# Second products of a two-layer pipeline taken out of the steps of the first products

## The chip, the core and the metric

The kernel runs on one core of a Trainium2 chip. TensorE (PE in the profile, its weight loads PEld) does the matrix products out of SBUF into PSUM; VectorE (DVE), ScalarE (ACT) and GpSimd (POOL) work on tiles in SBUF and PSUM; SyncE (SP) issues nearly all transfers. Each engine works through its own list of instructions in order, and semaphores tie the lists together. The metric is device time in microseconds (us), and less is better. Before the change three runs gave 1913.86, 1925.21 and 1925.63 us, with a median of 1925.21.

## The reference

Three stages, all in float32, over 8 sequences of 576 positions (4608 tokens, width 512):

```python
scores = scale * q @ k.T                  # 8 heads of 64
ret = scores * Dmat                       # Dmat = gamma[h] ** (i - j) for i >= j, else 0
x = ret @ v                               # 4608 x 512

h = x @ w_in                              # first MLP: 512 -> 2048
g = h * (1.0 / (1.0 + np.exp(-1.702 * h)))
x = g @ w_out                             # 2048 -> 512

h = x @ w_in2                             # second MLP
g = h - np.tanh(h)
out = g @ w_out2
```

## The kernel before

**Three passes.** A product of two float32 matrices is made of three: each operand is split into a high part in float32r and the rest, and the pairs high-high, high-low and low-high are added up in PSUM (`PASS`). A split costs one copy on ACT and one subtraction on DVE.

**Steps.** Tokens are cut into 9 blocks of 512, the 2048 inner columns into 16 groups of 128. One step of an MLP is one block and one group, 144 steps for each MLP and 288 in all (MLP 1 has 0 to 143, MLP 2 has 144 to 287). A step has a *first product* (x by w_in, 12 matmuls of 512 columns, `mm_in`, L419, or L618 and L632 in MLP 2), an *activation* (ACT and DVE, result in the tile `t`), a store of `t` to DRAM (`g_store`, L455), later a load of it (`g_load`, L463, tile `gl`), a split (`act_b`, ACT L468 and DVE L469, tile `g`) and a *second product* (g by w_out, four units of three matmuls, `mm_out`, L485 in MLP 1 and L487 in MLP 2). Its w_out rows come from DRAM (`wo_load`, L200, 512 KB, tile `wos`, three buffers). After 16 second products a block is done and `evac` copies the four PSUM accumulators out (L503).

**What runs beside what.** Retention (`attn_step`, a batch every other step) feeds the first product. The second product of step o runs in the program step of the first product s = o + 32, from s = 32 to s = 143. Beside it go the decoding of the weights from 64-bit floats (`dec_piece`), then `w2_prep`, which stores the combinations of w_in2 that are used later (DVE `ws` L563, POOL L585), and from s = 90 on nothing of the decoding is left. Then the first block of MLP 2 is multiplied plainly (`mm_std`, L618, 16 steps, activation `act_2`). The other 8 blocks go in four pairs, by a scheme with 7 half-size products in place of 8: for each of 8 groups q the parts 1, 6, 5, 2, 7, 3, 4 (`mm_part`, L632, 6 matmuls each) yield four h tiles. Parts 1 and 2 share the PSUM bank x, 5 and 3 bank y, 7 and 4 bank z, and 6 has bank w; x and w lie in one PSUM tile, `pat`. Part results are copied (m1, m7, h22 on ACT) and added (u2, h12, h21 on DVE, h22 on POOL). Between the parts `some(outs, n)` hands out n units of second products, 16 units (four steps) for each q, so that at the end 32 steps of second products remain. For each pair the operands of the next are made (`xo_prep`: POOL L640, ACT L543, DVE L544).

**Order.** The program is written in its final order, and a tile that is allocated takes the buffer that comes free. In a program step the loads for the second product come ahead: `out_loads(o)` asks for w_out and for `gl` of step o + 2, `act_b` is one step ahead, and `stores(2)` stores the activation of two steps ago:

```python
        out_loads(o)
        mm_in(s)
        if s % 2 == 0 and EARLY + BPB + (s - LAG) // 2 <= TILES * BPT:
            attn_step(EARLY + BPB + (s - LAG) // 2)
        dec_piece()
        act_a(s)
        act_b(o + 1)
        done.append(s)
        stores(2)
        for m in range(4):
            mm_out(o, m)
```

The tile `t` has three buffers, `gl` two, `g` two, and a first product's PSUM tile `h` two.

Of the kernel before, what the change touches and what calls it, by code (L numbers as in the profile page):

```python
# [17 lines left out]
P = 128  # L18
# [24 lines left out]
GDS = 6 * NF  # L43
# [5 lines left out]
def kernel(  # L49
# [16 lines left out]
    at_p = ctx.enter_context(tc.tile_pool(name="at", bufs=2))  # L66
# [10 lines left out]
    qt_sb = const.tile([P, KD, P], F32, name="qt_sb")  # L77
    mt_sb = const.tile([P, BPT, 2, 2, P], F32, name="mt_sb")
    mk_sb = const.tile([P, P], F32, name="mk_sb")
    jt_sb = const.tile([P, HEADS], F32, name="jt_sb")  # L80
    kt_sb = const.tile([P, 2, HEADS, 1], F32, name="kt_sb")
    gt_sb = const.tile([P, HP], F32, name="gt_sb")
# [3 lines left out]
    sbd = [const.tile([P, 2, P], F32, name=f"sbd{bt}") for bt in range(BPT)]  # L86
    s_sb = [const.tile([P, 2, HD], F32, name=f"s_sb{bt}") for bt in range(BPT)]
# [345 lines left out]
    def act_2(s, h):  # L433

        tt[s] = t = t_p.tile([P, BLK], F32, tag="t", name="t", bufs=3)
        sq = t_p.tile([P, BLK], F32, tag="e", name="sq")
        pl = t_p.tile([P, BLK], F32, tag="z", name="pl", bufs=3)
        if not marks:
            marks["t"] = at_p.tile([P, 4, BLK], F32, tag="at", name="marks")
            marks["n"] = 0  # L440
        small = marks["t"][:, marks["n"] % 4]
# [11 lines left out]
    def g_store(s):  # L453
        gd[s] = dram.tile([P, BLK], F32, tag=f"g{s % GDS}", name="gd")
        nc.sync.dma_start(out=gd[s], in_=tt.pop(s))  # L455

    def g_load(s):
        if s < (2 * NB - 2) * NF:
            t = t_p.tile([P, BLK], F32, tag="gl", name="gl")
        else:  # L460
            t = st_p.tile([P, BLK], F32, tag="stg", name="gl", bufs=3)
        gl[s] = t
        nc.sync.dma_start(out=t, in_=gd.pop(s))  # L463

    def act_b(s):
        t = gl.pop(s)
        gt[s] = g = g_p.tile([P, 2, BLK], F32R, tag="g", name="g")
        nc.scalar.activation(out=g[:, 0], in_=t, func=ACTF.Copy)  # L468
        nc.vector.tensor_tensor(out=g[:, 1], in0=t, in1=g[:, 0].bitcast(F32), op=ALU.subtract)  # L469
# [19 lines left out]
    def evac(s):  # L489
# [3 lines left out]
        if j >= NB - 2:  # L493
            o = at_p.tile([P, 4, BLK], F32, tag="at", name="o")
            parts = [o[:, m] for m in range(4)]
        else:
            parts = [p_p.tile([P, BLK], F32, tag="p", name="o") for m in range(4)]
        for m in range(4):
            r = (j - NB) * BLK + m * P
# [5 lines left out]

    def out_loads(o):
        if o + 2 < n_steps:
            wo_load(o + 2)
            last = (2 * NB - 2) * NF
            for u in (o + 2,) if o + 2 < last else (last, last + 1) if o + 2 == last else (o + 3,):  # L510
                if u < n_steps:
                    g_load(u)

    def out_units(first, last):

        for o in range(first, last):
            out_loads(o)
            if o + 1 < n_steps:
                act_b(o + 1)
            for m in range(4):  # L520
                mm_out(o, m)
                if m == 3:
                    if o % NF == NF - 1:
                        evac(o)
# [216 lines left out]
    for i in range(NF):  # L741
# [9 lines left out]
        if i == NF - 1:  # L751
            act_b(0)
# [8 lines left out]
        if NF - 5 <= i < NF - 3:  # L761
            wo_load(i - NF + 5)
            g_load(i - NF + 5)

    n_steps = 2 * NB * NF
# [13 lines left out]
    xo_tag += [f"wi{f}" for f in range(NF)] + ["ws", "ws"]  # L779
    for s in range(LAG, NB * NF):  # L780
        j, f = divmod(s, NF)
        o = s - LAG
        out_loads(o)
        mm_in(s)
        if s % 2 == 0 and EARLY + BPB + (s - LAG) // 2 <= TILES * BPT:
            attn_step(EARLY + BPB + (s - LAG) // 2)
        dec_piece()
        act_a(s)
        act_b(o + 1)
# [5 lines left out]
        if f == NF - 1:  # L795
            evac(o)
# [7 lines left out]
    outs = out_units(NB * NF - LAG, n_steps)  # L804
# [3 lines left out]
    for i in range(NF):  # L808
# [4 lines left out]
        some(outs, 1)  # L813
        act_2(s, h)
        done.append(s)
        stores(2)
        some(outs, 3)
# [8 lines left out]
    for p in range(pairs):  # L826
# [6 lines left out]
        for q in range(QS):  # L833
# [7 lines left out]

            x_ps, w_ps = pat[:, 0], pat[:, 1]
            mm_part(x_ps, q, 1, True)
            if late:
                late[0]()
            some(outs, 2)
            if late:
                late[1]()
            stores(2)
            ready()  # L850

            m1 = p_p.tile([P, BLK], F32, tag="p", name="m1")
            nc.scalar.activation(out=m1, in_=x_ps, func=ACTF.Copy)  # L853
            mm_part(w_ps, q, 6, True)
            some(outs, 2)
            u2 = p_p.tile([P, BLK], F32, tag="p", name="u2")
            nc.vector.tensor_tensor(out=u2, in0=w_ps, in1=m1, op=ALU.add)
            ready()
            y_ps = ps_h.tile([P, BLK], F32, tag="h", name="y")
            mm_part(y_ps, q, 5, True)  # L860
            some(outs, 2)
            if late:
                late[2]()
            stores(2)
            ready()

            h22 = p_p.tile([P, BLK], F32, tag="p", name="h22")
            nc.scalar.activation(out=h22, in_=y_ps, func=ACTF.Copy)  # L868
            nc.gpsimd.tensor_tensor(out=h22, in0=u2, in1=h22, op=ALU.add)  # L869
            mm_part(x_ps, q, 2, False)  # L870
            some(outs, 2)
            act_2(ids[0] + q, x_ps)
            done.append(ids[0] + q)
            ready()
# [3 lines left out]
            stores(2)  # L878
# [96 lines left out]
```

## Time and profile before

| | |
|---|---|
| median of three runs | 1925.21 us |
| profiled execution, device time | 1926.46 us |
| its span, first to last instruction | 1924.6 us |
| mean granted TensorE clock | 0.961 of full speed |
| busy: PE, DVE, ACT, POOL | 92%, 62%, 45%, 13% of the span |
| transfers | 514 MB, mean 267 GB/s |
| chain of waits, by engine | PE 50%, DMA 16%, DVE 16%, ACT 10% |

The page's busy share of PE counts a matmul from its issue to its end, and neighbours overlap; how fast PE really goes is seen in how many matmuls start in a stretch. The chain of waits is followed back from the last instruction: DMA, DVE and ACT have 42% of it, though PE is the engine with the most work.

### The profile page before, as it was taken

The page shows a single profiled execution, that of the slowest core. Times are in us where ns is not written, and L with a number is a line of the kernel's source. Part 1 is how long each engine was busy: PE and PEld are TensorE (multiplying, and loading weights), DVE is VectorE, ACT ScalarE, POOL GpSimd, SP SyncE. Part 2 cuts the span into 40 slices and gives each one's busy share as a digit, 9 for nine tenths or more (in the row PEclk, how much of TensorE's full clock was granted, in tenths as well). Part 3 has the DMA queues.
Part 4 walks back from the last instruction along what each step waited for, and adds up shares of the span by engine and source line. Part 5 has one row for each costly group of instructions (what it writes and reads, how often), then busy time and mean ns, then how long its engine had stood idle before and what let it go on. Part 6 is the DMA issues. An engine that isn't in the chain of part 4 may idle for free.

```text
span 1924.6 us, 24809 instructions
## 1 busy us (share of the span) xinstructions
PE 1764.3 (92%) x8714; PEld 1412.2 (73%) x8714; DVE 1184.0 (62%) x1837; ACT 872.3 (45%) x1587; POOL 252.5 (13%) x185
## 2 busy tenths in 40 slices
PE   7998999999999999999988897988888888988898
PEld 5786888888788888888766676766666666767677
DVE  6798865666633333334656787767766777766632
ACT  3344432343423233224554566555555656555522
POOL 4011000101011111000200211121111211111100
PEclk8999999999999999999989998999988998999999
DMA  6559998888989787889968776777677677777843
GB/s 238 170 196 331 368 328 294 283 317 298 322 282 306 261 284 267 274 274 367 387 247 293 246 256 243 252 241 255 232 250 261 238 239 243 268 251 242 324 147 110
DMA packets 176029, 514.23 MB, mean 267 GB/s; under 512 B 19873, under 2 KB 21025, under 8 KB 164385
## 3 DMA queue, kind: packets, MB, share of 16 engines
q1 hardware_dynamic: 164960, 493.69, 73.8%
q10 hardware_dynamic: 10944, 18.96, 2.6%
q8 instruction: 69, 1.13, 0.2%
q14 instruction: 56, 0.45, 0.1%
HBM read 380.45 MB, written 132.12 MB: 266 GB/s over the span
## 4 chain that ended last, share of the span: by engine, by line
PE 50%; DMA 16%; DVE 16%; ACT 10%; issue 6%; ACTq 0%; SPq 0%; POOL 0%; DVEq 0%; POOLq 0%
PE acc L485 17%; PE h L419 16%; DMA gl<-gd 11%; PE acc L487 6%; DVE g L469 4%; DMA gd<-t 4%; ACT pl L446 2%; DVE pl L449 2%; DVE pl L450 2%; ACT sq L445 2%; PE pat L632 2%; PE pat L287 2%; DVE t L444 2%; ACT t L443 1%; ACT g L468 1%
## 5 line engine op out<-in xcount | busy, mean ns | idle before, releaser
L485 PE MATMUL acc<-g,wos 128*128 128x512 f32 x1728 | 431.6, 397 | 20.4 <-DVE g L469 11.5
L487 PE MATMUL acc<-wos,g 128*128 128x512 f32 x1398 | 380.2, 408 | 55.0 <-DVE g L469 38.4
L485 PEld LDWEIGHTS acc<-g,wos 128*128 128x128 f32 x1728 | 322.8, 190 | 99.2 <-DVE g L469 15.3
L419 PE MATMUL h<-xh,wi 128*128 128x512 f32 x1152 | 380.8, 394 | 6.4 <-DVE t L429 4.8
L487 PEld LDWEIGHTS acc<-wos,g 128*128 128x128 f32 x1398 | 275.1, 198 | 133.6 <-DVE g L469 51.8
L469 DVE TENSOR_TENSOR g<-gl,g 128x512 fp32r<-128x512 f32 x288 | 258.8, 906 | 181.2 <-ACT g L468 180.6
L468 ACT ACTIVATE g<-gl 128x512 fp32r<-128x512 f32 x288 | 180.1, 626 | 310.8 <-PE acc L487 143.1
L419 PEld LDWEIGHTS h<-xh,wi 128*128 128x128 f32 x1152 | 218.9, 190 | 55.0 <-DVE t L429 5.4
L419 PE MATMUL h<-xl,wi 128*128 128x512 f32 x576 | 226.6, 393 | 0.7 <-DVE xl L353 0.7
L429 DVE SCALAR_TENSOR_TENSOR t<-t,h 128x512 f32<-128x512 f32 x144 | 98.5, 684 | 193.7 <-ACT t L428 193.1
L632 PE MATMUL pat<-xo,wq 128*128 128x512 f32 x576 | 159.6, 415 | 53.2 <-ACT m L853 53.2
L632 PEld LDWEIGHTS pat<-xo,wq 128*128 128x128 f32 x576 | 110.7, 197 | 89.3 <-ACT m L853 67.0
L428 ACT ACTIVATE t<-h 128x512 f32<-128x512 f32 x144 | 85.2, 593 | 190.5 <-DMA gd<-t 100.0
L449 DVE SCALAR_TENSOR_TENSOR pl<-pl,sq 128x512 f32<-128x512 f32 x144 | 99.5, 691 | 99.1 <-ACT pl L446 98.9
L451 DVE COPY_PREDICATED t<-marks,pl 128x512 f32<-128x512 int32 x144 | 134.1, 931 | 14.8
L244 POOL TENSOR_TENSOR at<-at,qt_sb 128x512 f32<-128x512 f32 x35 | 47.6, 1361 | 625.0 <-DMA at<-in_attn_dram 517.7
L419 PEld LDWEIGHTS h<-xl,wi 128*128 128x128 f32 x576 | 109.4, 190 | 23.4 <-DVE xl L353 1.0
L353 DVE TENSOR_TENSOR xl<-pat,xh 128x256 fp32r<-128x256 f32 x61 | 25.8, 423 | 163.0 <-ACT xh L352 163.0
L112 ACT ACTIVATE e<-e,ebias 128x512 int32<-128x512 int32 x64 | 46.3, 724 | 173.9 <-DVE e L110 173.9
L869 POOL TENSOR_TENSOR h<-u,h 128x512 f32<-128x512 f32 x32 | 46.7, 1460 | 577.5 <-ACT h L868 577.5
L632 PE MATMUL z<-xo,wq 128*128 128x512 f32 x384 | 111.8, 432 | 0.0
L446 ACT ACTIVATE pl<-sq,abias 128x512 f32<-128x512 f32 x144 | 104.2, 723 | 4.7
(92 smaller groups left out, 2121.7 us busy)
## 6 DMA issues: line engine op xcount, KB each, us to landing
wos<-wd SPq DMA_DIRECT2D x262, 512.0 KB, 4.8
gd<-t SPq DMA_DIRECT2D x288, 256.0 KB, 5.1
gl<-gd SPq DMA_DIRECT2D x288, 256.0 KB, 4.4
wq<-wq SPq DMA_DIRECT2D x48, 1024.0 KB, 7.5
at<-in_attn_dram SPq DMA_DIRECT2D x33, 1024.0 KB, 6.3
stg<-in_w_dram SPq DMA_DIRECT2D x64, 512.0 KB, 6.8
wq<-wq SPq DMA_DIRECT2D x32, 768.0 KB, 9.1
wd<-ws SPq DMA_DIRECT2D x32, 512.0 KB, 6.5
```

Of the source, the lines that this page charges most:

```text
L244: eng.tensor_tensor(out=qv, in0=qv, in1=qt_sb[:, hp], op=ALU.mult)
L419: nc.tensor.matmul(h, lhsT=win[f][:, a, k], rhs=xs[b][:, k], start=(n == 0), stop=(n == 3 * KD - 1))
L428: nc.scalar.activation(out=t, in_=h, func=ACTF.Tanh, scale=0.851)
L429: nc.vector.scalar_tensor_tensor(out=t, in0=t, scalar=1.0, in1=h, op0=ALU.add, op1=ALU.mult)
L446: nc.scalar.activation(out=pl, in_=sq, func=ACTF.Square, bias=abias)
L449: nc.vector.scalar_tensor_tensor(out=pl, in0=pl, scalar=CB, in1=sq, op0=ALU.add, op1=ALU.mult)
L451: nc.vector.copy_predicated(out=t, mask=small.bitcast(I32), data=pl)
L468: nc.scalar.activation(out=g[:, 0], in_=t, func=ACTF.Copy)
L469: nc.vector.tensor_tensor(out=g[:, 1], in0=t, in1=g[:, 0].bitcast(F32), op=ALU.subtract)
L485: nc.tensor.matmul(acc[m], lhsT=wo[:, a, c], rhs=g[:, b], start=first, stop=last)
L487: nc.tensor.matmul(acc[m], lhsT=g[:, a, c], rhs=wo[:, b], start=first, stop=last)
L632: nc.tensor.matmul(ps, lhsT=wq[q][t][:, o, a, k], rhs=xo[i][k][:, b], start=first and n == 0, stop=n == 5, skip_group_check=True,)
```

## The change

1. The second products become one generator, `out_units()`, from step 0. The program steps up to s = 89 (`PAUSE = 90`) still hand out four units each; the 54 steps from s = 90 to 143 hand out none.
2. The 54 missing steps are made up later: 22 steps instead of 16 beside `mm_std`, and 22 units instead of 16 (5.5 steps) for each q of the pairs. 32 steps remain at the end, as before.
3. In the pairs the parts go 1, 5, 7, 6, 2, 3, 4, each followed by three or four units; the copies of banks x, y and z (m1, h22, m7) are issued right after their part; u2 and both POOL additions follow part 6; the activations of the last group are spread over the next.
4. Once retention is over (s = 126), its tables and buffers give way to a pool that adds three buffers for `t`, two for `gl`, one for `g` and four for outputs. From then on `gl` is loaded four steps ahead, and `act_b` is two ahead.
5. `marks`, a mask of `act_2`, has two rows in place of four, and each stored activation has a DRAM tile of its own.

```diff
+    second = {}
+    turns = {"t": 0, "gl": 0, "g": 0}
+    def turn(what):
+        shape, dt, n = {"t": ([P, BLK], F32, 3), "gl": ([P, BLK], F32, 2), "g": ([P, 2, BLK], F32R, 2)}[what]
+        i = turns[what]
+        turns[what] += 1
+        more = {"t": 3, "gl": 2, "g": 1}[what]
+        if second and i % (n + more) >= n:
+            return second["pool"].tile(shape, dt, tag=what + "2", name=what, bufs=more)
...
     def out_loads(o):
         if o + 2 < n_steps:
             wo_load(o + 2)
...
+        while n_g[0] <= min(o + (4 if second else 2), n_steps - 1):
+            g_load(n_g[0])
+            n_g[0] += 1
+    def out_split(o):
+        while n_b[0] <= min(o + (2 if second else 1), n_steps - 1):
+            act_b(n_b[0])
+            n_b[0] += 1
+    def out_units():
+        for o in range(n_steps):
             out_loads(o)
+            out_split(o)
             for m in range(4):
                 mm_out(o, m)
...
+    outs = out_units()
     for s in range(LAG, NB * NF):
         j, f = divmod(s, NF)
         o = s - LAG
-        out_loads(o)
+        if s < PAUSE:
+            out_loads(o)
         mm_in(s)
...
         act_a(s)
-        act_b(o + 1)
+        if s < PAUSE:
+            out_split(o)
         done.append(s)
         stores(2)
-        for m in range(4):
-            mm_out(o, m)
+        if s < PAUSE:
+            some(outs, 4)
...
         mm_std(s, h, s % NF)
-        some(outs, 1)
+        some(outs, 2)
         act_2(s, h)
         done.append(s)
-        stores(2)
-        some(outs, 3)
+        stores(3)
+        some(outs, 3 + half_)
...
             mm_part(x_ps, q, 1, True)
+            m1 = copied(x_ps, "m1")
             if late:
+                h21 = added(late["z"], late["u2"], "h21")
+            some(outs, 3)
             if late:
+                act(late["id"][1] + QS, late["h22"])
             y_ps = ps_h.tile([P, BLK], F32, tag="h", name="y")
             mm_part(y_ps, q, 5, True)
+            h22 = copied(y_ps, "h22")
+            ready()
+            some(outs, 3)
             if late:
+                act(late["id"][0] + QS, late["h12"])
             z_ps = ps_h.tile([P, BLK], F32, tag="h", name="z")
             mm_part(z_ps, q, 7, True)
+            m7 = copied(z_ps, "m7")
+            ready()
             some(outs, 3)
+            mm_part(w_ps, q, 6, True)
+            u2 = added(w_ps, m1, "u2")
+            nc.gpsimd.tensor_tensor(out=h22, in0=u2, in1=h22, op=ALU.add)
+            nc.gpsimd.tensor_tensor(out=h22, in0=h22, in1=m7, op=ALU.add)
             ready()
+            some(outs, 3)
+            if late:
+                act(late["id"][1], h21)
+            mm_part(x_ps, q, 2, False)
+            ready()
+            some(outs, 3)
+            act(ids[0] + q, x_ps)
             mm_part(y_ps, q, 3, False)
+            h12 = added(y_ps, u2, "h12")
+            ready()
+            some(outs, 3)
             mm_part(z_ps, q, 4, False)
+            some(outs, 4)
```

`copied` and `added` are one ACT copy and one DVE addition out of PSUM into a new tile; `act` is `act_2`, then `stores(3)`.

Three places where the change moves instructions. First SP's list, two program steps, s = 50 and 51, before (wd_1583 and wd_1645 are rows of w_out, `gd` stored activations):

```order
L200 DMA wos_2779<-wd_1583 128x1024
L463 DMA gl_2781<-gd_1036 128x512
L236 DMA at_2812<-in_attn_dram 128x2048
L159 DMA wr_2816<-z_2647 128x512
L100 DMA stg_2818<-in_w_dram 128x512
L455 DMA gd_2828<-t_2706 128x512
L200 DMA wos_2847<-wd_1645 128x1024
L463 DMA gl_2849<-gd_1085 128x512
L455 DMA gd_2871<-t_2758 128x512
```

and two steps, s = 48 and 49, of the list after the change:

```order
L202 DMA wos_2699<-wd_1538 128x1024
L476 DMA gl_2701<-gd_916 128x512
L457 DMA gd_2747<-t_2613 128x512
L202 DMA wos_2749<-wd_1538 128x1024
L161 DMA wr_2767<-z_2609 128x512
L102 DMA stg_2769<-in_w_dram 128x512
L202 DMA wos_2773<-wd_1553 128x1024
L476 DMA gl_2775<-gd_965 128x512
L457 DMA gd_2801<-t_2659 128x512
L202 DMA wos_2803<-wd_1553 128x1024
```

Each row of w_out is now loaded twice in a step, since `out_loads(o)` is called by the loop and again by the generator: 320 loads of `wos` in place of 262, the 58 more in the steps s = 32 to 89. Only the second of the two tiles is read. In the built program the load that is read, or the one ahead of it, waits for the second product of the same step o; before the change the only load waited for that of step o - 1.

Second, PE's list for most of one group q of a pair, before (acc is a second product, pat bank x or w):

```order
L632 MATMUL pat<-xo,wq 128x512 x6
L487 MATMUL acc_13390<-wos,g 128x512 x3
L487 MATMUL acc_13394<-wos,g 128x512 x3
L632 MATMUL pat<-xo,wq 128x512 x6
L487 MATMUL acc_13419<-wos,g 128x512 x3
L487 MATMUL acc_13423<-wos,g 128x512 x3
L632 MATMUL y<-xo,wq 128x512 x6
```

and after the change, from part 1 to part 2 of a group:

```order
L651 MATMUL pat<-xo,wq 128x512 x6
L500 MATMUL acc_11099<-wos,g 128x512 x3
L500 MATMUL acc_11103<-wos,g 128x512 x3
L500 MATMUL acc_11107<-wos,g 128x512 x3
L651 MATMUL y<-xo,wq 128x512 x6
L500 MATMUL acc_11132<-wos,g 128x512 x3
L500 MATMUL acc_11099<-wos,g 128x512 x3
L500 MATMUL acc_11103<-wos,g 128x512 x3
L651 MATMUL z<-xo,wq 128x512 x6
```

Part 6, which stood two units behind part 1 in the same PSUM tile, now stands behind parts 5 and 7 and nine units. Third, DVE's list in one group of a pair after the change, from the activation of h12 to the start of that of bank x:

```order
L446 TENSOR_TENSOR t<-h_9988,t 128x512
L451 SCALAR_TENSOR_TENSOR pl<-pl,sq 128x512
L452 SCALAR_TENSOR_TENSOR pl<-pl,h_9988 128x512
L453 COPY_PREDICATED t<-marks,pl 128x512
L482 TENSOR_TENSOR g<-gl,g 128x512
L877 TENSOR_TENSOR u_10140<-pat,m_10038 128x512
L446 TENSOR_TENSOR t<-h_10040,t 128x512
L451 SCALAR_TENSOR_TENSOR pl<-pl,sq 128x512
L452 SCALAR_TENSOR_TENSOR pl<-pl,h_10040 128x512
L453 COPY_PREDICATED t<-marks,pl 128x512
L482 TENSOR_TENSOR g<-gl,g 128x512
L446 TENSOR_TENSOR t<-pat,t 128x512
```

u2 stands between the activations of h12 and h21, and in the built program part 2 waits for it, because banks x and w are one tile.

## Rows read from the trace of the kernel before

**Rows 1.** Windows of the five stages: busy us and instructions by engine.

```profile
core 0: us, PE busy (x) PEld busy (x) DVE busy (x) ACT busy (x) POOL busy (x), PEclk, DMA share, GB/s
180.00:554.50 374.50, 371.25 (x2154) 303.78 (x2153) 238.68 (x451) 138.45 (x276) 34.32 (x28) 1.00 0.90 316
554.50:886.60 332.10, 332.10 (x1806) 273.31 (x1805) 116.09 (x211) 103.39 (x208) 41.64 (x47) 1.00 0.82 282
886.60:979.30 92.70, 89.61 (x386) 72.72 (x385) 57.19 (x84) 52.21 (x89) 10.24 (x4) 0.98 1.00 378
979.30:1821.00 841.70, 718.60 (x2873) 562.33 (x2872) 601.61 (x777) 476.39 (x810) 133.80 (x76) 0.93 0.73 253
1821.00:1924.60 103.60, 93.46 (x394) 75.25 (x392) 30.70 (x45) 30.99 (x51) 0.00 (x0) 0.96 0.41 135
```

**Rows 2.** Timeline of PE, three entries in the pairs: start us, us, engine, line.

```profile
1002.28 1.52 PE L632 MATMUL z<-xo,wq 128*128 128x512 f32 x6
1003.64 2.20 PE L485 MATMUL acc<-g,wos 128*128 128x512 f32 x9
1005.68 1.52 PE L632 MATMUL y<-xo,wq 128*128 128x512 f32 x6
```

**Rows 3.** Waits of PE, 980 to 1830 us.

```profile
PE pat L632 <- ACT m L853: 53.2, 32, 4.8
PE acc L487 <- DVE g L469: 38.4, 28, 2.1
PE acc L487 <- ACT g L468: 15.9, 14, 4.0
```

**Rows 4.** Windows in the first stage and the plain block, columns as above.

```profile
200.00:250.00 50.00, 50.00 (x313) 41.42 (x312) 39.75 (x78) 21.67 (x42) 4.59 (x4) 1.00 1.00 377
250.00:300.00 50.00, 50.00 (x290) 41.09 (x289) 28.63 (x54) 18.20 (x37) 3.81 (x3) 1.00 0.90 304
900.00:950.00 50.00, 47.41 (x203) 38.59 (x202) 29.20 (x42) 25.24 (x42) 7.52 (x3) 0.97 1.01 397
```

**Rows 5.** Line L200 (loads of w_out), 180 to 554 us, issue to landing.

```profile
DMA to landing us min/median/max: 3.2/6.3/10.7
```

**Rows 6.** Waits of ACT, 554.5 to 886.6 us: total us, times, longest.

```profile
ACT t L428 <- DMA gd<-t: 57.9, 12, 6.3
```

**Rows 7.** Line L455 (stores of t), 554.5 to 886.6 us, issue to landing.

```profile
DMA to landing us min/median/max: 3.7/5.5/8.5
```

**Rows 8.** Timeline of POOL, 560 to 575 us.

```profile
566.24 1.29 POOL L244 TENSOR_TENSOR at<-at,qt_sb 128x512 f32<-128x512 f32 x1 [23.45 <-DMA at<-in_attn_dram]
567.50 1.04 POOL L250 TENSOR_TENSOR at<-at,kt_sb 128x512 f32<-128x512 f32 x1
568.50 3.49 POOL L585 TENSOR_TENSOR wr<-wr 128x256 f32<-128x256 f32 x4
```

**Rows 9.** Page, part 6: count, KB each, median us from issue to landing.

```profile
at<-in_attn_dram SPq DMA_DIRECT2D x33, 1024.0 KB, 6.3
```

**Rows 10.** Groups of DVE, 980 to 1820 us: count, busy, mean ns, idle before.

```profile
L469 DVE TENSOR_TENSOR g<-gl,g 128x512 fp32r<-128x512 f32 x129 | 144.0, 1132 | 106.9 <-ACT g L468 106.3
L451 DVE COPY_PREDICATED t<-marks,pl 128x512 f32<-128x512 int32 x127 | 121.2, 954 | 13.1
L449 DVE SCALAR_TENSOR_TENSOR pl<-pl,sq 128x512 f32<-128x512 f32 x126 | 86.9, 690 | 76.6 <-ACT pl L446 76.4
L450 DVE SCALAR_TENSOR_TENSOR pl<-pl,h 128x512 f32<-128x512 f32 x94 | 65.1, 692 | 3.2
L444 DVE TENSOR_TENSOR t<-h,t 128x512 f32<-128x512 f32 x94 | 64.4, 685 | 2.9 <-ACT t L443 2.8
```

**Rows 11.** The group of L469 in the second stage, 554.5 to 886.6 us.

```profile
L469 DVE TENSOR_TENSOR g<-gl,g 128x512 fp32r<-128x512 f32 x54 | 38.7, 716 | 0.0
```

**Rows 12.** Groups of POOL, pairs.

```profile
L883 POOL TENSOR_TENSOR h<-h,m 128x512 f32<-128x512 f32 x32 | 53.5, 1670 | 150.5 <-ACT m L882 145.2 <-DMA wos<-wd 5.2
```

**Rows 13.** Line L200, pairs, issue to landing.

```profile
DMA to landing us min/median/max: 3.1/3.9/12.8
```

More of the change, by code (lines that the diff above doesn't have):

```diff
@@ L492, in evac @@
             x2_d[j] = dram.tile([P, KD, BLK], F32, tag=f"x2{j}", name="x2")
[L493 to L497, printed above, removed]
+        parts = []
         for m in range(4):
+            if second:
+                parts.append(second["pool"].tile([P, BLK], F32, tag="o", name="o", bufs=4))
+            else:
+                parts.append(p_p.tile([P, BLK], F32, tag="p", name="o"))
             r = (j - NB) * BLK + m * P
@@ L508, in out_loads @@
             wo_load(o + 2)
[L509 to L516, printed above, removed]
+        while n_g[0] <= min(o + (4 if second else 2), n_steps - 1):
[7 more added lines that the diff above has]
+        for o in range(n_steps):
             out_loads(o)
-            if o + 1 < n_steps:
-                act_b(o + 1)
+            out_split(o)
             for m in range(4):
                 mm_out(o, m)
-                if m == 3:
-                    if o % NF == NF - 1:
-                        evac(o)
+                if m == 3 and o % NF == NF - 1:
+                    evac(o)
                 yield
@@ L840, in ready, with act, copied, added @@
                         wo_stay(f)
+            def act(s, h):
+                act_2(s, h)
+                done.append(s)
+                stores(3)
+            def copied(ps, name):
+                t = p_p.tile([P, BLK], F32, tag="p", name=name)
+                nc.scalar.activation(out=t, in_=ps, func=ACTF.Copy)
+                return t
+            def added(ps, t, name):
+                o = p_p.tile([P, BLK], F32, tag="p", name=name)
+                nc.vector.tensor_tensor(out=o, in0=ps, in1=t, op=ALU.add)
+                return o
@@ L864 @@
[L864 to L874, printed above, removed]
+                act(late["id"][0] + QS, late["h12"])
             z_ps = ps_h.tile([P, BLK], F32, tag="h", name="z")
@@ L883 @@
-            nc.gpsimd.tensor_tensor(out=h22, in0=h22, in1=m7, op=ALU.add)
-            mm_part(y_ps, q, 3, False)
-            some(outs, 2)
-            h12 = p_p.tile([P, BLK], F32, tag="p", name="h12")
-            nc.vector.tensor_tensor(out=h12, in0=y_ps, in1=u2, op=ALU.add)
-            act_2(ids[1] + q + QS, h22)
-            done.append(ids[1] + q + QS)
+            some(outs, 3)
[3 more added lines that the diff above has]
+            ready()
@@ L897 @@
                     wo_stay(f)
-            late_h = {}
-            def late_0(u2=u2, z_ps=z_ps, late_h=late_h):
-                late_h[0] = p_p.tile([P, BLK], F32, tag="p", name="h21")
-                nc.vector.tensor_tensor(out=late_h[0], in0=z_ps, in1=u2, op=ALU.add)
-            def late_1(h12=h12, s=ids[0] + q + QS):
-                act_2(s, h12)
-                done.append(s)
-            def late_2(late_h=late_h, s=ids[1] + q):
-                act_2(s, late_h[0])
-                done.append(s)
-            late = (late_0, late_1, late_2)
+            late = {"z": z_ps, "u2": u2, "h22": h22, "h12": h12, "id": [n + q for n in ids]}
             u = p * QS + q + 2
@@ L916 @@
                 wq_load(u % QS, False)
-    for l in late:
-        l()
+    h21 = added(late["z"], late["u2"], "h21")
+    act(late["id"][1] + QS, late["h22"])
+    act(late["id"][0] + QS, late["h12"])
+    act(late["id"][1], h21)
     stores(0)
```

85 lines of the change are left out of this document (35 added, 50 removed).

## The prediction

> **What bounds the kernel now.** I read the windows by stage first, since an average over stages with different limits says little [rows 1]. Stage 1 (180 to 554.5 us) holds the program steps s = 32 to 89, stage 2 (to 886.6) s = 90 to 143, stage 3 (to 979.3) the plain block of MLP 2, stage 4 (to 1821) the four pairs, stage 5 what is left. What to see there is how many matmuls a stage has for its length. For their pace comes PE's timeline: nine start between 1003.64 and 1005.68 us, so one takes 0.2267 us when nothing waits, and a product of 12 takes 2.72 [rows 2]. Stage 2 has 54 steps of 24, 1296 x 0.2267 = 293.8 us; I give the other 38.3 of its 332.1 us to the 18 retention batches, 2.1 each. PE bounds it, and it loses nothing. Stage 3 has 384, 87.1 of 92.7 us, with transfers at a share of 1.00 and 378 GB/s: it stands at both limits. Stage 4 has 32 groups q of 42 + 48 = 90: 2880 x 0.2267 = 652.9 of 841.7 us. It loses 189 us, 5.9 in each group, at a mean granted clock of 0.93 where stages 1 and 2 have 1.00. So only stage 4 has much slack on PE, and the waits say what it waits for [rows 3]: part 6 for the copy m1, once in each group (53.2 us), and second products for their split on DVE (38.4) or ACT (15.9), 107.5 in all. The rest of the 189 I put down to matmuls at the lower of the clock's two levels (1.2 against 2.4 GHz) around such stops.
>
> **The change part by part.** No matmul is added: 54 second products leave stage 2, 6 go to stage 3 and 48 to stage 4. The sum is made against the profiled execution, span 1924.6 us.
>
> *Stage 1, the doubled loads.* 58 more loads of 0.524 MB are 30.4 MB beside 316 GB/s x 374.5 us = 118.3 MB. How fast transfers can go here no row shows. At the 397 GB/s of one stretch, 148.7 MB take 374.6 us, nothing more; if they stay at the 304 GB/s of the quiet part they take 489, +115 [rows 1, 4]. I take the 378 GB/s of stage 3, the longest stretch at a share of 1.00: 393, +19. Besides, the load that is read now starts when the second product of its own step ends. Until it is read there are two first products, one second product and one batch, 3 x 2.72 + 2.1 = 10.3 us, and landings take 3.2 to 10.7 with a median of 6.3 [rows 5]: mostly covered, but behind 0.524 MB more (1.4 us) the late ones are not; 7 us for that. Together +26, ends 0 and +115. The Trainium skill (DMA: Bandwidth & Descriptors, section Bandwidth) says that about 358 GB/s of HBM bind a core's loads; by it stage 1 would last 415 us, +41, but the 378 and 397 of the rows lie above it, so the measurement decides.
>
> *Stage 2, first products alone.* 648 matmuls go: -147 us, if PE still bounds it. What covered the rest shrinks with the step, from 6.1 us to 3.8 with retention and 2.72 without. First, ACT waits for a store already now, 12 times and 4.8 us on average, with no cost, because PE was busy [rows 6]. A buffer of `t` is needed again three steps on; a store behind a load of retention input lands 5.5 to 8.5 us after its issue [rows 7], tanh and multiplication follow (0.7 each), so 6.9 to 9.9 us, while PE comes to the bank after two first products and a batch, 7.5: 1.5 us at each of 9 such loads, 13. Second, POOL's four subtractions of `w2_prep` (3.49 us) stand behind the scaling of that load (1.29 + 1.04) in POOL's list [rows 8], which waits for its landing (6.3 [rows 9]); three times they fall into the same step, and ACT's copy of their result stands ahead of the next tanh. 12.1 us and the ACT and DVE passes behind them make about 14, against three steps, some 10: 4 us, three times, 12. Third, in the 18 steps without retention a buffer of `t` goes round in 1.4 + 1.4 (the `ws` pass that SP waits for) + 5.5 = 8.3 us against 3 x 2.72: 5. So -147 + 30 = -117; ends -147 and, with all landings at 8.5, -85.
>
> *Stage 3.* 456 matmuls, 103.4 us; transfers 35.0 + 6 x 0.786 = 39.7 MB, 105 us at 378 GB/s. With the 6 us that the stage now loses beyond PE, 111: +18, ends +11 and +30 (twice that loss, and the skew of both limits).
>
> *Stage 4.* 32 x 108 x 0.2267 = 783.5 us for PE. DVE has 601.6 + 48 more splits of 1.132 = 656 [rows 1, 10], 84%; transfers 213.0 + 37.7 MB, 663 us at 378 GB/s. So PE is longest, but two others stand near it. Part 6 no longer waits for m1, since two parts and nine units lie between; splits are two steps ahead, loads four, so the three waits of rows 3 should go. What is late next: part 2 for u2, the ends of 11 blocks, and the last group of a pair, which makes ten operand halves. I leave a third of today's loss, 66 us (2.1 in each group): 850, +8. Ends are none (783.5, -58) and today's 5.9 in each group (972, +130). Moving the copies, the larger `stores(3)` and two rows of `marks` I cost at nothing: ACT, with 476 us of work in 842, hides them; without that cover a copy is 0.6 us in each part.
>
> *Stage 5* keeps its 32 steps: 0.
>
> Sum: +26 - 117 + 18 + 8 = -65, a span of 1859.6 and 1861 us with the 1.9 around it. The profiled execution (1926.46) lies 1.3 above the median, so 1861 is 3.3% below 1925.21.
>
> **The rivals.** A, the forecast, 0.50, from 1825 to 1905 by itself.
>
> B, 0.24: stage 4 runs at PE's pace but for the three heavy groups (20 us): 46 less, 1815, and 1790 where stage 1 pays nothing too. For it: stages 1 and 2 show PE without loss beside transfers at 316 GB/s; against: DVE had 64% there.
>
> C, 0.12: the doubled loads bound stage 1. SP stops for the second product of the step, then everything issued behind it comes late. From 7.7 us a step (445 us, +71) the change is no longer faster by 1%; at +115 it gives 1950. For it: the share is already 0.90; against: the landings of rows 5.
>
> D, the other side, 0.08: DVE's list makes PE wait in the pairs. u2 stands behind the activation of h12 (0.685 + 0.690 + 0.692 + 0.954 = 3.0 us [rows 10]) and a split, and part 2 comes nine matmuls, 2.04 us, behind part 6. If DVE comes one activation late, PE waits 3.0 + 0.7 - 2.0 = 1.7 us in each group; two late, 4.7, and from there on (149 lost, 1944) it is slower by 1%; at 5.9 it gives 1983. For it: 84% of DVE in list order; against: from part 1 to the end of part 6 there are 45 matmuls, 10.2 us, for two activations, two or three splits and an addition, 9.0 to 10.1. The split on DVE takes 1132 ns in the pairs but 716 in stage 2 [rows 10, 11], where POOL does less; a POOL addition of the pairs takes 1670 [rows 12]. The Trainium skill (SBUF — State Buffer, section Who interferes with whom) says that a DVE instruction with two SBUF inputs and a GpSimd one that reads SBUF shut each other out for a whole instruction; the rows agree. By it the second of the two POOL additions, which now stand together, would hold up a split by 1.7 us in each group, 53 in all: 1914, the same path as D at a lower price, and within its chance.
>
> E, 0.06: w_out comes late in the pairs. It is asked for two steps ahead, 8 units and at least two parts, 36 matmuls, 8.2 us; landings have a median of 3.9 but reach 12.8 [rows 13], behind the 1.8 MB of the next group's weights. Half of the 4.6 us once in each group is 74: 1935.
>
> That the change does not do what it says the lists exclude, but for the doubled loads.
>
> **How the numbers follow.** About 1% (19 us) is what a measurement of this kernel can tell from no change, so faster means below 1906 and slower above 1944. Faster: A 0.48, B 0.24, C 0.05, D and E 0.02: 0.79. Same: A 0.02, C 0.05, D 0.02, E 0.03: 0.12. Slower: C 0.02, D 0.05, E 0.02: 0.09. The range 1785 to 1925 leaves out the best of B (0.08) and the worse parts of C, D and E (0.12).
>
> **What would show it.** In the changed profile: stage 1 near 400 us with a transfer share near 1.00; s = 90 to 143 in some 215 us, with ACT's tanh waiting for stores and PE for `h` banks; the plain block in 111; the pairs in 850, 26.5 us a group, clock nearer 1.00, no wait on m1, and waits of `pat` on u2 and of `acc` on g below 50 us together. Stage 1 above 445 us or pairs above 920 would prove the sum wrong.

## Result and profile after

The changed kernel takes 1835.65 us (median of four runs, 1827.62 to 1836.59), the kernel before 1923.15 us beside it (four runs, 1913.86 to 1925.63). The ratio is 0.954, with a 95% interval of 0.950 to 0.959: 4.6% faster. The forecast was 1861, range 1785 to 1925. The profiled execution took 1836.18 us, its span is 1834.4.

First the windows by stage, with the same columns as [rows 1] and the same places in the program as bounds: s = 90, the start of the plain block, part 1 of the first group, the end of the last part 4.

```profile
180.00:582.90 402.90, 385.75 (x2157) 307.56 (x2157) 234.71 (x446) 137.14 (x272) 32.37 (x28) 0.98 0.97 362
582.90:783.60 200.70, 189.69 (x1157) 153.24 (x1156) 82.34 (x157) 66.63 (x140) 41.23 (x47) 0.98 0.71 247
783.60:897.30 113.70, 107.10 (x458) 87.16 (x457) 67.05 (x97) 60.55 (x103) 9.94 (x4) 0.97 0.94 350
897.30:1727.20 829.90, 800.78 (x3446) 651.40 (x3446) 616.79 (x819) 503.40 (x862) 137.84 (x76) 0.99 0.87 303
1727.20:1834.40 107.20, 92.47 (x396) 75.44 (x395) 30.70 (x46) 31.85 (x52) 0.00 (x0) 0.94 0.46 152
```

Set against [rows 1], the stages changed by +28.4, -131.4, +21.0, -11.8 and +3.6 us, in all -90.2. Read against the matmuls they hold, at 0.2267 us each [rows 2], the pairs lost 189 us before (841.7 - 652.9) and lose 46 now (829.9 - 783.5), with 576 more matmuls in them: 1.45 us per group in place of 5.9. The first stage has grown though its matmuls are the same, and its transfer share has gone from 0.90 to 0.97.

What PE waits for in the pairs (us in total, times, longest), which answers to [rows 3]:

```profile
PE acc L498 <- DMA wos<-wd: 10.1, 4, 3.6
PE pat L651 <- DVE u L877: 8.2, 6, 3.6
PE acc L500 <- DMA wos<-wd: 6.4, 2, 3.2
PE acc L498 <- ACT o L516: 2.0, 2, 1.8
```

The waits for m1, for the split on DVE and for the split on ACT (107.5 us in [rows 3]) are gone. The rows of w_out (`wos`) and u2 are late in their place, 24.7 us in all. How an undisturbed group looks shows in PE's timeline (start us, us, engine, line), from part 1 by 5, 7 and 6 to part 2, parts and second products in turn, with no idle time noted at any of them:

```profile
1136.56 1.52 PE L651 MATMUL pat<-xo,wq 128*128 128x512 f32 x6
1137.92 2.20 PE L498 MATMUL acc<-g,wos 128*128 128x512 f32 x9
1139.96 1.52 PE L651 MATMUL y<-xo,wq 128*128 128x512 f32 x6
1141.32 2.20 PE L498 MATMUL acc<-g,wos 128*128 128x512 f32 x9
1143.36 1.52 PE L651 MATMUL z<-xo,wq 128*128 128x512 f32 x6
1144.72 2.20 PE L498 MATMUL acc<-g,wos 128*128 128x512 f32 x9
1146.76 1.52 PE L651 MATMUL pat<-xo,wq 128*128 128x512 f32 x6
1148.12 2.20 PE L498 MATMUL acc<-g,wos 128*128 128x512 f32 x9
1150.16 1.52 PE L651 MATMUL pat<-xo,wq 128*128 128x512 f32 x6
```

In the first stage ACT's tanh waits for the store that frees its buffer (waits of ACT, 180 to 582.9 us); in the kernel before the same wait was 39.6 us, 17 times:

```profile
ACT t L430 <- DMA gd<-t: 130.5, 39, 8.5
```

These stores now land 7.8 us after their issue (median), before 6.5. PE itself was idle for 17.2 us of this stage, waiting for splits and for w_out; before, for 3.3 us. The other half of the growth is slower matmuls: for the same number PE's busy time rose by 14.5 us, at a mean granted clock of 0.98 in place of 1.00.

### The profile page after: what moved, and what is told of

Read it like the earlier page. It is cut to its first block, busy times and chain, and to the rows that moved or that the text cites. A ratio compares the mean times of both kernels' runs of the same rounds, so it can differ in the third digit from the quotient of the medians.

```text
span 1834.4 us, 24895 instructions
## 1 busy us (share of the span) xinstructions
PE 1732.3 (94%) x8714; PEld 1397.2 (76%) x8714; DVE 1173.0 (64%) x1837; ACT 871.5 (48%) x1587; POOL 253.6 (14%) x185
## 4 chain that ended last, share of the span: by engine, by line
PE 60%; DMA 20%; DVE 10%; ACT 5%; issue 3%; SPq 1%; ACTq 1%; DVEq 0%
PE acc L500 17%; PE acc L498 13%; PE h L421 10%; DMA gd<-t 9%; DMA wos<-wd 7%; PE pat L651 6%; PE y L651 4%; PE z L651 4%; PE h L637 1%; DVE t L431 1%; PE pat L500 1%; DVE g L482 1%; DVE p L312 1%; ACT t L430 1%; ACT o L516 1%
## 5 line engine op out<-in xcount | busy, mean ns | idle before, releaser
L498 PE MATMUL acc<-g,wos 128*128 128x512 f32 x1728 | 439.9, 400 | 36.3 <-DMA wos<-wd 18.3
L500 PE MATMUL acc<-wos,g 128*128 128x512 f32 x1398 | 346.0, 392 | 7.1 <-DMA wos<-wd 6.4
L482 DVE TENSOR_TENSOR g<-gl,g 128x512 fp32r<-128x512 f32 x288 | 211.5, 738 | 170.9 <-ACT g L481 166.0
L500 PEld LDWEIGHTS acc<-wos,g 128*128 128x128 f32 x1398 | 264.2, 190 | 65.4 <-issue 7.1
L431 DVE SCALAR_TENSOR_TENSOR t<-t,h 128x512 f32<-128x512 f32 x144 | 98.6, 685 | 214.6 <-ACT t L430 214.1
L451 DVE SCALAR_TENSOR_TENSOR pl<-pl,sq 128x512 f32<-128x512 f32 x144 | 120.3, 835 | 85.4 <-ACT pl L448 83.9
L651 PE MATMUL pat<-xo,wq 128*128 128x512 f32 x576 | 153.6, 404 | 9.6 <-DVE u L877 8.2
L905 POOL TENSOR_TENSOR h<-u,h 128x512 f32<-128x512 f32 x32 | 53.6, 1675 | 710.9 <-DVE u L877 645.2
L453 DVE COPY_PREDICATED t<-marks,pl 128x512 f32<-128x512 int32 x144 | 129.1, 897 | 16.3 <-DVE pl L452 0.9
L446 DVE TENSOR_TENSOR t<-h,t 128x512 f32<-128x512 f32 x112 | 89.6, 800 | 24.7 <-ACT t L445 24.7
L449 ACT ACTIVATE marks<-sq,sbias 128x512 f32<-128x512 f32 x144 | 102.0, 709 | 0.0
```

The lines of the kernel that those rows point to most:

```text
L431: nc.vector.scalar_tensor_tensor(out=t, in0=t, scalar=1.0, in1=h, op0=ALU.add, op1=ALU.mult)
L449: nc.scalar.activation(out=small, in_=sq, func=ACTF.Relu, bias=sbias, scale=-1.0)
L451: nc.vector.scalar_tensor_tensor(out=pl, in0=pl, scalar=CB, in1=sq, op0=ALU.add, op1=ALU.mult)
L453: nc.vector.copy_predicated(out=t, mask=small.bitcast(I32), data=pl)
L498: nc.tensor.matmul(acc[m], lhsT=wo[:, a, c], rhs=g[:, b], start=first, stop=last)
L500: nc.tensor.matmul(acc[m], lhsT=g[:, a, c], rhs=wo[:, b], start=first, stop=last)
```

## Experiments

The theory after the result: the pairs gained because the new **order** of the parts and the deeper **reach** (reload four ahead, split two ahead) took away the waits of [rows 3]; the **moved** second products are fill, work that PE has to do in one stage or another; and the doubled loads give back some 28 us. The rival: the six further units in each group are themselves the cover, that is, the work that keeps PE busy until late results arrive, and order and reach matter little.

**One load of each row.** The base of what follows: `e1_single` leaves the unread load out.

```diff
-        if o + 2 < n_steps:
+        if o + 2 < n_steps and o + 2 not in wos:
             wo_load(o + 2)
```

> The changed kernel with each row of w_out loaded once per step (the second load of s = 32 to 89 left out). Theory 1: the 28 us that the first stage grew by (374.5 to 402.9) are the doubled loads, by share of the transfers and by the stores and loads queued behind them; the stage returns to 375 to 380 us, the others stay, in all 1808 us (1800 to 1815). Rival: the stage is longer for another reason (second products handed out by the generator, loads of stored activations in another place); it stays above 393 us and the kernel at 1827 or more.

Measured: 1804.62 us (six runs, 1799.69 to 1810.65), ratio to before 0.940 (0.936 to 0.943). Its windows of the first two stages and the pairs:

```profile
180.00:556.50 376.50, 374.35 (x2157) 305.85 (x2158) 239.49 (x448) 138.80 (x276) 35.70 (x28) 1.00 0.89 313
556.50:751.20 194.70, 186.94 (x1158) 151.39 (x1156) 81.97 (x155) 66.20 (x139) 41.73 (x47) 1.00 0.71 246
864.00:1691.00 827.00, 798.59 (x3446) 649.90 (x3445) 615.43 (x817) 502.98 (x861) 134.23 (x76) 0.99 0.88 304
```

The first stage is back at 376.5, and stage 2 gives another 6 us. The doubled loads cost 31 of about 118 us that the change could have gained.

**Products back in the steps.** `e3_in_steps`, on the same base, changes the counts alone.

```diff
-PAUSE = 90
+PAUSE = 144
...
-        some(outs, 2)
+        some(outs, 1)
         act_2(s, h)
...
-        some(outs, 3 + half_)
+        some(outs, 3)
```

and in a group of the pairs 2, 2, 2, 3, 2, 2, 3 units in place of 3, 3, 3, 3, 3, 3, 4.

> Single loads, and the second products back in their steps: four units in every step to s = 143, 16 beside the plain block, 16 units per group of a pair; the new part order, the extra buffers and the deeper reload stay. Theory 1: moving second products is only fill, the loss of the pairs went with the new order and the deeper reload. Then stage 2 is back at 332 us without loss, the plain block at 94, the pairs at 653 + 49 = 702 us, and the kernel takes about 1790 us, 19 less than with the products moved (1775 to 1805). Rival (fill): the six further units per group cover the activations and copies; without them the pairs keep at least two thirds of their 189 us, 780 us, and the kernel takes 1868 or more.

Measured: 1815.49 us (1810.57 to 1819.40), ratio 0.944 (0.941 to 0.947). Stage 2 and the pairs:

```profile
554.90:887.50 332.60, 332.60 (x1805) 273.31 (x1804) 116.19 (x211) 103.92 (x209) 41.64 (x47) 1.00 0.83 284
981.00:1703.70 722.70, 675.32 (x2873) 547.07 (x2873) 575.84 (x773) 464.97 (x808) 132.51 (x76) 0.98 0.84 289
```

The time lies between the 1790 of the theory and the 1868 of the rival. The pairs lose 69.8 us (722.7 - 652.9) with order and reach (and the added buffers) alone, in place of 189 before and 43.5 (827.0 - 783.5) with the moved products as well. What the fill covers is above all the activation that frees bank x for the next part 1. This is PE's largest wait in the pairs here (1.5 us in the base):

```profile
PE pat L651 <- DVE pl L452: 24.0, 13, 2.3
```

So both theories have a part, and their sizes are far apart: order and reach are worth 119 us in the pairs, the fill 26, of which stages 2 and 3 give back 12 (194.7 us against 332.6 less 648 matmuls, 185.7; and 112.8 for the plain block against 93.5 and 72 matmuls more, 109.8). As a whole, moving the products is worth 11 us (1815.49 against 1804.62; of the six runs of each, only the longest of the one, 1810.65, reaches the shortest of the other, 1810.57).

**Reach, order, and both undone.** `e4_shallow` takes back the reach, `e5_old_order` the order, each on the base of single loads.

```diff
-        while n_g[0] <= min(o + (4 if second else 2), n_steps - 1):
+        while n_g[0] <= min(o + 2, n_steps - 1):
...
-        while n_b[0] <= min(o + (2 if second else 1), n_steps - 1):
+        while n_b[0] <= min(o + 1, n_steps - 1):
```

> Single loads, and the reach of before: activations reloaded two steps ahead and split one ahead; the buffers, the order and the moved products stay. Theory 1: second products wait for their split again as they did before (38.4 + 15.9 us, now for 176 steps of the pairs in place of 128: 75 us), 1880 us (1850 to 1900). Rival: the new order alone frees DVE and ACT in time, reach brings nothing: within 10 us of the single-load kernel (1808).

```diff
             mm_part(x_ps, q, 1, True)
-            m1 = copied(x_ps, "m1")
...
+            nc.scalar.activation(out=m1, in_=x_ps, func=ACTF.Copy)
+            mm_part(w_ps, q, 6, True)
+            some(outs, 3)
...
             mm_part(y_ps, q, 5, True)
-            h22 = copied(y_ps, "h22")
...
-            z_ps = ps_h.tile([P, BLK], F32, tag="h", name="z")
-            mm_part(z_ps, q, 7, True)
-            m7 = copied(z_ps, "m7")
...
-            mm_part(w_ps, q, 6, True)
-            u2 = added(w_ps, m1, "u2")
...
+            z_ps = ps_h.tile([P, BLK], F32, tag="h", name="z")
+            mm_part(z_ps, q, 7, True)
+            some(outs, 4)
```

The activations, additions and stores of the pairs stand as before the change too.

> Single loads, and the pairs' parts, copies, additions and stores as before (1, 6, 5, 2, 7, 3, 4), with 22 units per group spread 3, 3, 3, 3, 4, 3, 3; moved products, buffers and reach stay. Theory 1: part 6 waits for the copy m1 again, 1.66 us per group less the 0.68 that one unit more covers, 31 us, with slower matmuls around each stop another 10 to 30: 1850 to 1870 us. Rival (fill): three units cover the copy, the order is worth nothing, within 10 us of 1808.

`e7_move_alone` has both edits, so that of the change only the moved products, the generator, the buffers and the small `marks` are left.

> Single loads, the pairs' order of before and the reach of before together: of the change only the moved products, the generator and the extra buffers are left. Theory (order and reach each cost their own waits): the losses add, 1805 + 72 + 71 = 1948 us, so moving alone makes the kernel slower than before. Rival (both waits fall into the same stops of PE): about 1900, so moving alone would still gain 1%.

Measured: 1876.93 us without the reach (ratio 0.976, 0.972 to 0.980), 1875.29 without the order (0.976, 0.972 to 0.980), 1983.43 without both (1.033, 1.028 to 1.039). The first was forecast, the others came out 5 and 35 us above. The windows of the pairs for the three, in that order:

```profile
875.00:1757.10 882.10, 818.04 (x3447) 647.86 (x3446) 604.33 (x815) 502.15 (x862) 131.06 (x76) 0.98 0.83 286
867.40:1769.60 902.20, 828.69 (x3449) 667.67 (x3448) 621.52 (x820) 504.95 (x865) 131.12 (x76) 0.96 0.81 280
875.00:1873.80 998.80, 862.11 (x3449) 683.79 (x3449) 603.38 (x817) 503.05 (x862) 127.65 (x76) 0.93 0.74 253
```

And rows of PE there (count, busy us, mean ns, idle before), in the same order:

```profile
L500 PE MATMUL acc<-wos,g 128*128 128x512 f32 x1333 | 341.2, 397 | 35.1 <-DVE g L482 16.1 <-ACT g L481 14.3 <-ACT o L516 4.5
L498 PE MATMUL acc<-g,wos 128*128 128x512 f32 x770 | 199.9, 398 | 24.7 <-DVE g L482 11.3 <-ACT g L481 9.5 <-ACT o L516 3.5
```

```profile
L651 PE MATMUL pat<-xo,wq 128*128 128x512 f32 x576 | 165.5, 427 | 60.1 <-ACT m L876 60.1
```

```profile
L500 PE MATMUL acc<-wos,g 128*128 128x512 f32 x1336 | 353.1, 409 | 31.6 <-DVE g L482 20.3 <-ACT g L481 11.1 <-ACT o L516 0.2
L651 PE MATMUL pat<-xo,wq 128*128 128x512 f32 x576 | 173.6, 443 | 88.4 <-ACT m L876 88.3
```

Without the reach the splits are late (51.2 us), without the order m1 is (60.1), each as in [rows 3]; either costs about 71 us. Of the order, no run separates the sequence of the parts from the place of the copies. Without both the losses more than add: 179 us above the base, not 143, and **moving the products, without order and reach, makes the kernel 3.3% slower than before** (no run has the generator and the buffers by themselves). The pairs then take 998.8 us and lose 215. They stand 172 us above the base, where the two single losses (55 and 75) make 130. Of the 42 us between, 28 are idle time of PE, and the row of `pat` shows where: with the split late as well, m1 comes later still (88.3 against 60.1). The other 14 are busy time, slower matmuls: the mean of `pat` is 400 ns in the base, 427 without the order and 443 without both, and the mean granted clock of the pairs goes from 0.99 to 0.96 and 0.93.

**What the doubled loads cost, and why.** `e2_before_twice` puts the second load into the kernel before; `e12_two_bufs` keeps single loads, but gives them the late place and the late wait of the doubled ones.

```diff
         stores(2)
+        if s < 90:
+            wo_load(o + 2)
         for m in range(4):
             mm_out(o, m)
```

> The kernel before, with each row of w_out loaded a second time in the steps s = 32 to 89 (58 loads more, only the second tile is read) and nothing else changed. Theory: the doubled load costs in any list what it cost in the changed kernel, its first stage goes from 374.5 to 403 us and the kernel to 1950 (1940 to 1958). Rival (the price comes from the doubled load together with the other order of the changed list): at most 10 us, 1932 or less.

```diff
-        t = wos[o] = wos_p.tile([P, 2, DM], F32R, tag="wos", name="wos")
+        third = o >= PAUSE - LAG and o % 3 == 2
+        t = wos[o] = wos_p.tile([P, 2, DM], F32R, tag="wos3" if third else "wos", name="wos", bufs=1 if third else 2)
...
-            out_loads(o)
+            out_loads(o, False)
```

(with False, `out_loads` leaves the load of w_out to the generator)

> Single loads in the place where the second of the doubled loads stood, and two buffers for w_out in place of three up to s = 89: the load that is read waits for the second product of its own step, as in the changed kernel, but no byte is loaded twice. The sum of the prediction (19 us for the bytes, 7 for the later wait): first stage 383, kernel 1811. Rival 1, the wait is all of the 26: stage 400, kernel 1830. Rival 2, only the second transfer and its place among the transfers under way cost anything: stage 376, kernel 1805.

Measured: 1946.43 us for the kernel before with doubled loads, ratio 1.014 (1.010 to 1.017), 28.4 us above the 1918.08 of before beside it; and 1807.15 us with the late wait alone (0.942, 0.938 to 0.945), 2.5 above the base. The first stages, first of the one, then of the other:

```profile
182.00:573.57 391.57, 375.26 (x2133) 301.60 (x2132) 230.48 (x439) 133.69 (x266) 30.01 (x26) 0.99 0.99 370
```

```profile
185.00:561.29 376.29, 373.77 (x2156) 305.61 (x2154) 233.82 (x444) 135.93 (x269) 32.78 (x28) 1.00 0.88 307
```

(These two kernels begin the stage at other times, so the windows start elsewhere; from the first second product to s = 90 they take 398.1 and 377.7 us, the kernel before 375.4, which is 22.7 and 2.3 less.) The 2.5 us of the late wait lie within the spread of the base's runs. The price goes with the second transfer, not with the late wait: with it the share is 0.97 to 0.99, and ACT's tanh waits for stores 39 times, for 121.7 us in the one and 130.5 in the changed kernel; with the late wait alone it is 36.7 us, 13 times. One thing stays open. With doubled loads SP also stands at a load of w_out until an earlier one has landed, with everything behind it in its list; in the changed kernel's first stage:

```profile
SPq L202 <- DMA wos<-wd: 83.8, 39, 5.5
```

No run has this wait without the bytes, so how the price divides between the two isn't shown.

**POOL's additions on DVE.** `e6_adds_dve` moves the two additions to h22.

```diff
-            nc.gpsimd.tensor_tensor(out=h22, in0=u2, in1=h22, op=ALU.add)
-            nc.gpsimd.tensor_tensor(out=h22, in0=h22, in1=m7, op=ALU.add)
+            nc.vector.tensor_tensor(out=h22, in0=u2, in1=h22, op=ALU.add)
+            nc.vector.tensor_tensor(out=h22, in0=h22, in1=m7, op=ALU.add)
```

> Single loads, and the two additions to h22 in each group moved from POOL to DVE. In the single-load kernel's pairs the split takes 741 ns, the activation's three passes over SBUF 840, 864 and 847, against 716, 685, 690 and 692 in rows where POOL did not add at that time. Theory (POOL's additions hold up DVE instructions that read two tiles of SBUF): the four means fall back to 716 to 730 and to 685 to 700, 55 us of DVE's 615 go, the 64 additions bring 44, so DVE stays near 604; the time stays within 8 us of 1805, as PE bounds the pairs. Rival (the passes are long because transfers write SBUF beside them): the means stay, DVE reaches 660 us and the kernel loses 5 to 20 us.

Measured: 1802.26 us (0.939, 0.935 to 0.942), the same as the base. Groups of DVE in the pairs (count, busy us, mean ns, idle before), of the base and of this kernel:

```profile
L482 DVE TENSOR_TENSOR g<-gl,g 128x512 fp32r<-128x512 f32 x176 | 129.6, 741 | 102.5 <-ACT g L481 102.2
L451 DVE SCALAR_TENSOR_TENSOR pl<-pl,sq 128x512 f32<-128x512 f32 x126 | 108.9, 864 | 63.6 <-ACT pl L448 62.1
L452 DVE SCALAR_TENSOR_TENSOR pl<-pl,pat 128x512 f32<-128x512 f32 x32 | 22.0, 687 | 1.1
```

```profile
L482 DVE TENSOR_TENSOR g<-gl,g 128x512 fp32r<-128x512 f32 x177 | 123.2, 697 | 116.2 <-ACT g L481 116.2
L451 DVE SCALAR_TENSOR_TENSOR pl<-pl,sq 128x512 f32<-128x512 f32 x126 | 93.0, 738 | 65.2 <-ACT pl L448 63.2
L905 DVE TENSOR_TENSOR h<-u,h 128x512 f32<-128x512 f32 x32 | 22.2, 692 | 1.1
```

DVE is given 64 additions of 692 ns, 44 us, and its busy time in the pairs still falls from 615.4 to 600.5 us: its other work takes 59 us less, where 55 were expected. The timeline of the base shows how: in one group POOL's two additions run from 1112.33 to 1115.34 us, the split beside them takes 1.33 us and the next activation's subtraction 1.79; the pass of L451 behind them takes 0.68. In the base's pairs all 69 splits and activation passes of DVE that took over 1 us ran beside an instruction of POOL; the 107 passes of L451 that ran beside none took 0.69 us on average, the 19 others 1.84. The means don't come back all the way without the additions (738 against 690), because POOL still has 32 us of `xo_prep` there: 3 of the 126 passes of L451 ran beside it and took 2.7 us each, the others 0.69. (The pass that reads `pat` from PSUM keeps its 687 ns, but none of its 32 ran beside POOL.) So POOL's additions do hold up DVE, and it costs the kernel nothing that can be measured: PE bounds the pairs.

**What was still lost.** `e8_store_early` stores one step earlier in stage 2, `e9_wos4` gives w_out a fourth buffer, `e10_both` does both, `e11_u2_later`, on top of that, moves one unit from behind part 4 to behind part 6.

```diff
-        stores(2)
+        stores(2 if s < PAUSE else 1)
```

> Single loads, and from s = 90 on each activation is stored one step earlier (one is kept back in place of two). Theory: what stage 2 loses (194.7 us against 185.7 of before less 648 matmuls) is tanh waiting for the store of its buffer (41 us of ACT, 7.7 of PE for h); the stage falls to 187 to 190 us, the kernel to 1798. Rival: SP then stands at the younger activation and sends the retention inputs and the passes of ws later; stage 2 stays or grows, 1805 to 1815.

```diff
+    def wos_tile():
+        n_wos[0] += 1
+        if second and n_wos[0] % 4 == 3:
+            return second["pool"].tile([P, 2, DM], F32R, tag="wos2", name="wos", bufs=1)
+        return wos_p.tile([P, 2, DM], F32R, tag="wos", name="wos")
...
-        more = {"t": 3, "gl": 2, "g": 1}[what]
+        more = {"t": 2, "gl": 2, "g": 1}[what]
...
-        if o + 2 < n_steps and o + 2 not in wos:
-            wo_load(o + 2)
+        for u in range(o + 2, o + (4 if second else 3)):
+            if u < n_steps and u not in wos:
+                wo_load(u)
```

> Single loads, and from s = 126 on a fourth buffer for w_out with loads three steps ahead (for the room, t has five buffers in place of six). Theory: PE's 16 us of waits for w_out in the pairs (5 times, up to 4.2 us) come from issue behind the second product that frees the buffer; they go, pairs 827 to about 812, kernel 1790. Rival: these loads are late because of the weights and inputs queued at the same time, and a longer list does not help: within 4 us of 1805.

> Single loads, stores one step earlier from s = 90 on, and the fourth buffer for w_out with loads three steps ahead: the two gains stand in different stages (7 us in stage 2, 11 in the pairs and the plain block) and add, 1786 us (1781 to 1790). Rival: t with five buffers in place of six takes the first gain back, 1793.

```diff
             ready()
-            some(outs, 3)
+            some(outs, 4)
             if late:
                 act(late["id"][1], h21)
...
             mm_part(z_ps, q, 4, False)
-            some(outs, 4)
+            some(outs, 3)
```

> As the last kernel, with four units in place of three between part 6 and part 2 and three in place of four behind part 4. Theory: part 2 waits for u2 (15.3 us, 9 times, in the kernel with four w_out buffers), 0.68 us more of cover each time takes half of it and the slower matmuls behind: 1778 us. Rival: DVE is late by an activation and a split there, as much as 3.8 us, 0.68 does nothing, and the next group's part 1 comes 0.68 earlier to the bank: within 3 us of the last kernel.

Measured: 1796.92 (ratio 0.935, 0.932 to 0.938), 1793.14 (0.934, 0.930 to 0.937), 1784.85 (0.929, 0.927 to 0.932) and 1782.45 us (0.929, 0.926 to 0.931). The first three came within 4 us of their forecasts; of the last the rival was right. Waits of ACT and of PE in stage 2, of the base and then with the early store:

```profile
ACT t L430 <- DMA gd<-t: 41.1, 11, 5.8
PE h L421 <- DVE t L431: 7.7, 9, 1.4
```

```profile
ACT t L430 <- DMA gd<-t: 3.1, 1, 3.1
PE h L421 <- DVE t L431: 1.4, 1, 1.4
```

Stage 2 falls from 194.7 to 187.4 us, 2 above its matmuls and retention batches. With the fourth buffer PE waits for w_out no more, and u2 is next; the waits of PE in the pairs, of `e10_both` and of `e11_u2_later`:

```profile
PE pat L660 <- DVE u L886: 15.1, 10, 3.6
PE pat L660 <- DVE pl L461: 1.7, 2, 0.8
```

```profile
PE pat L660 <- DVE u L886: 9.6, 6, 4.0
PE pat L660 <- DVE pl L461: 5.9, 6, 1.5
```

The two gains add. The last edit takes 5.5 us from the wait for u2 and gives 4.2 to the next part 1; its 2.4 us can't be told from nothing. The best kernel, `e11_u2_later`, is 7.1% below before and 53 us below the change.

## Why the prediction was right, and where it was not

The direction and the main mechanism were right; the gain, 65 us in the sum, was 90. The errors of stages 2 and 4 (14 and 20 us) have one sign, those of the others (2, 3 and 4) the other.

**Stage 1** (+26 forecast, +28.4 measured) was right in its sum by luck, as its two parts erred against each other. The late wait, put at 7 us, costs some 2.5 alone, so the second transfer, put at 19, costs about 26. The step that failed is the pace taken for the transfers, 378 GB/s: the stage ran at 362 with a share of 0.97 (370 in the kernel before with doubled loads). The Trainium skill (DMA: Bandwidth & Descriptors, section Bandwidth) gives about 358 GB/s as what binds a core's loads, as its share with both cores of a pair streaming. This kernel runs on one core, so the 362 measured over 400 us, though near that figure, doesn't show that limit at work.

**Stage 2** (-117, measured -131.4). The first of the three losses, 13 us of tanh waiting for stores and PE for `h` at nine places, is there: PE waited 11.0 us in nine waits, and storing earlier takes nearly all of it away. The second, 12 us behind POOL's subtractions of `w2_prep`, failed: ACT waited for POOL's result 1.5 us in the whole stage. The third, 5 us in the 18 steps without retention, failed too. SP does wait for the `ws` passes, 71.2 us in 26 waits, but neither ACT nor PE waits on a store once retention is over: from there on `t` has six buffers, where the sum counted three. (By its own numbers, 8.3 us against 3 x 2.72, the term would have been under 1 us.) Some 15 us were lost in place of 30, and 6 of these came with the doubled loads, since single loads give stage 2 in 194.7.

**Stage 3** (+18, measured +21.0) was right.

**Stage 4** (+8, measured -11.8). That m1, splits and reloads would cease to be late, and that u2 and the rows of w_out would be late next, was right. What failed is the size of the rest: a third of the former loss, 66 us, was a choice, and it was 46. The pairs stand between the forecast and rival B (803.5 us for the pairs; 829.9 measured). Of the former loss, too, more was waiting than the prediction read from [rows 3]: PE was idle for 123.1 of the 841.7 us [rows 1], not 107.5, which leaves 66 and not 81 for slower matmuls.

**Rival C** had the place right and the price wrong: the share did reach 0.97, but for 28 us, where from 71 on the gain would have been under 1%. **Rival D's** place was right (part 2 behind u2), its price not: 8.2 us in six waits, where one in each group was priced. Its sentence on the Trainium skill (SBUF — State Buffer, section Who interferes with whom) is borne out by the experiment on POOL's additions: DVE's long passes are those beside POOL. But the split was held up less than before, its mean falling from 1132 ns [rows 10] to 741 with single loads; the activation's passes stand beside the additions now. What this took from DVE cost PE nothing that can be measured, where 53 us had been priced. **Rival E** was right in kind: 16.5 us of waits for w_out, not 74.

The prediction's account by stages hides one thing. It reads as if the gain were stage 2's 54 second products, taken into slack of the pairs. That slack was not there to be filled: filled without the new order and the reach, the kernel took 61 us more than before. Order and reach, with their buffers, made the gain, 119 us in the pairs, with the products left where they were; the move is worth 11 on top.

## What to carry to other kernels

Idle time of an engine is a place for more work only if one knows what it waits for there; with the cause left in, more work beside it met the same stops here, and one late part made the next later. So take the waits away first, and only then move work. When two places of a program call the same loader, count the loads in the list: 58 transfers that nobody reads cost some 30 us here, in a stage whose share was 0.90 without them.

## What was not expected of the hardware

- Over some 400 us at a share of 0.97 to 0.99 the transfers moved 362 to 370 GB/s, less than the 377 and 397 of stretches of 50 us [rows 4].
- The time in which POOL's additions hold up DVE does not go away by order, it moves: the split had 1132 ns and the activation's pass 690 [rows 10], then the split 741 and the pass 864 with single loads; only without the additions on POOL both fell (697 and 738). A split that runs beside no instruction of POOL takes 0.69 us in the pairs of both kernels.
- Two kinds of stops cost more together than apart (215 us of loss in the pairs, against 98.6 and 118.7 for each kind and 43.5 for neither), with the mean granted clock at 0.93, 0.98, 0.96 and 0.99.
